# Attention block of a fused kernel: q kept per head with zero rows for the other head, q–k products over 112 rows, a state of 48 columns per pair

## Chip, cores and metric

The kernel runs on one core of a Trainium2 chip. The metric is the time of one execution on the device in microseconds (us). The core has five engines that run side by side, each with its own queue of instructions that it takes strictly in order: PE (TensorE, matrix products into PSUM), DVE (VectorE), ACT (ScalarE), POOL (GpSimd) and SP (here only issuing DMAs). Engines wait for each other through semaphores. PSUM has eight banks; all eight are in use here.

## The reference

Two stages. The first is linear attention with a decaying state, for 4 batches, 8 heads, 768 steps and 48 features per head:

```python
for t in range(S):
    state = alpha[:, :, t, :, None] * state + np.einsum('bhd,bhe->bhde', k[:, :, t], v[:, :, t])
    y[:, :, t] = np.einsum('bhd,bhde->bhe', q[:, :, t], state)
```

The second takes y, laid out as 3072 rows (batch and step) of 384 (heads and features), through a layer with 2048 hidden units:

```python
h = x @ w_in
r = np.maximum(h, 0.0)
g = s * (r * r) + b
return (g @ w_out).astype(np.float32)
```

Inputs and output are fp32. The products in the kernel take bf16 operands and sum in fp32.

## The kernel before

**Tiling.** The steps are cut into 24 blocks of 128 (six per batch, `n` from 0 to 23; `c = n % 6` is the place in the batch). The recurrence is turned into products within a block plus a state carried from block to block. The eight heads are handled as four pairs (`NP = 4`). A pair's features lie at 0 to 47 for the even head and 64 to 111 for the odd head, so that a transposed pair takes 112 rows, of which 48 to 63 are unused.

**One block goes through these functions**, in this order:

- `ln(n)` (L186, ACT): the logarithm of alpha. `vcast(n)` (L189, POOL): v to bf16.
- `cum(n)` (L195 to L211): PE adds the logarithms up over the steps (L195); ACT takes exp of the negative sums (`bi_sb`, L206) and of the sums (`b_sb`, L207). The decay over the whole block, `blast`, comes from PE and ACT for the first five blocks, and otherwise through DRAM by three small DMAs (`decay`).
- `qk(n)` (L223, L224, DVE): k times `bi_sb`, q times `b_sb`, in bf16.
- `tr(n)` (L229 to L237): eight transposes on PE, four pairs of q and four of k, into one bank, `ct_ps`, which `cum` uses too; then one DVE copy of 112x1024 from that bank to `qkT`.
- `amat(n)` (L244, L252): for each pair and head, one product of k and q over that head's 48 rows (0 to 47 or 64 to 111), 128 columns, eight in all. Those of even heads go to one bank (`a_ps[0]`), those of odd heads to another. DVE multiplies each bank with the triangular mask (`am_a`, `am_b`).
- `yp(n)` (L263, L272, L283, L290): y is the sum of the state's part (four products of 112 rows, 96 columns, with the state of the block before, `sd_sb`; none for `c = 0`) and of eight products of `am` and v (48 columns each). Then four products of k and v (96 columns per pair) give the block's addition to the state in `p_ps`. ACT copies y to bf16.
- `st(n)` (L331 to L343): DVE adds the carried state `sc_sb` to `p_ps` (`t1_sb`, 112x384). POOL multiplies with the decay: two instructions for the two heads of the pairs, which write the diagonal 48x48 parts of `sd_sb` in bf16 (its other parts stay at zero from the start), and one of 112x384 for `sc_sb` in fp32. The 96 columns of a pair hold 48 for the even and 48 for the odd head; the parts that mix the two heads are computed and not used.
- `xt(n)` (L311, L317): three transposes of y on PE, and a copy on ACT into `xd_all`.
- The second stage, in four quarters `u`: `mp` (L359, PE, 12 products with w_in of 128 columns into one of two banks `h_ps`), `rl` (L373, relu on ACT), `sq` (L380, square on DVE), and `mm2` (L397, PE, four products with w_out of 384 columns into `o_ps`). In the text these are also called by their names in the list: `m` is `mp`, `rl` and `sq`; `mr` is the first two; `o` is `mm2`. The output of the first 14 blocks is copied out by ACT (L406) and gets its bias later on DVE (L436); that of the others gets it at once on DVE (L410). Blocks 0 and 1 go through the second stage as one group with 256 columns.

**The order is written out by hand.** Every engine's queue has its instructions in the order in which the calls are made. For the first blocks the calls stand in a list; `busy` is filler work on PE that keeps its clock up. From the list, around blocks 1 and 2:

```python
(tr, 1), (ln, 2), (xt, 0), (vcast, 2), (cum, 2), (busy, 1), (amat, 1),
(busy, 3), (yp, 1), (qk, 2), (st, 1), (load_w_in, 1), ..., (busy, 1), (tr, 2), (ln, 3), (xt, 1), (vcast, 3), (cum, 3), (busy, 1), (amat, 2),
(busy, 3), (yp, 2), (qk, 3), (st, 2), (tr, 3), (xt, 2), (mr, 0, 0), (amat, 3), (mr, 0, 1), (mr, 1, 0), (sq, 0, 0), (weights_out,),
```

From block 4 on each call has a due position, with 8 units per block: `cum`, `tr` and `amat` of block `n` run 14.8, 10.8 and 7.9 units ahead of its `yp` in the middle of the run, and the four quarters of the second stage 2.5 to 14.5 units behind it.

**Loads.** SP issues the loads of alpha, k, q and v (192 KB each per block). POOL issues four loads of w_in that convert to bf16: the first behind `st(0)`, three behind `st(1)`. `weights_out` writes one element of `w_out_st` with DVE (L474) so that the loads of w_out, issued by SP (L136), come behind it. w_out is cast in four parts (L143 on DVE, L151 on ACT).

Of the kernel before, what the change touches and what calls it, by code (L numbers as in the profile page):

```python
# [8 lines left out]
FP32 = mybir.dt.float32  # L9
BF16 = mybir.dt.bfloat16  # L10
AF = mybir.ActivationFunctionType
ALU = mybir.AluOpType

@with_exitstack
def kernel(
# [12 lines left out]
    nc = tc.nc  # L28

    B, H, S, D = q.shape  # L30
    C = 128
    NCH = S // C
    NP = H // 2
# [14 lines left out]
    sb = ctx.enter_context(tc.tile_pool(name="sb", bufs=1))  # L48
# [5 lines left out]
    t_ps = ct_ps.bitcast(BF16).rearrange("a (x p t) -> a x p t", x=2, p=NP)  # L54
# [8 lines left out]
    def ring(name, shape, dtype, n):  # L63
        return [sb.tile(shape, dtype, name=f"{name}{i}") for i in range(n)]
# [30 lines left out]
    xd_all = sb.tile([128, UNITS, KT * C], BF16, name="xd_all")  # L95
# [130 lines left out]
    def tr(n):  # L226
        for x, t in ((0, qb_sb[n % 2]), (1, kb_sb[n % 3])):
            for p in range(NP):
                nc.tensor.transpose(  # L229
                    out=t_ps[0:112, x, p, :],  # L230
                    in_=t.rearrange("a h d -> a (h d)")[:, 128 * p : 128 * p + 112],
                    identity=ident,
                )
        nc.vector.tensor_copy(  # L234
            out=qkT_sb[n % 2][0:112].rearrange("a x p t -> a (x p t)"),
            in_=t_ps[0:112].rearrange("a x p t -> a (x p t)"),
        )  # L237

    def amat(n):
        qkT = qkT_sb[n % 2]  # L240
        for p in range(NP):
            for e in range(2):
                r0 = 64 * e
                nc.tensor.matmul(  # L244
                    out=a_ps[e][:, p, :],
                    lhsT=qkT[r0 : r0 + 48, 1, p, :],
                    rhs=qkT[r0 : r0 + 48, 0, p, :],
                    start=True,
                    stop=True,
                )  # L250
        for e in range(2):
            nc.vector.tensor_tensor(out=am_sb[e][n % 2], in0=a_ps[e], in1=mask4, op=ALU.mult)  # L252

    group_of = []
    for g, sz in enumerate(GROUPS):
# [3 lines left out]
    def yp(n):  # L259
        c = n % NCH  # L260
        if c > 0:
            for p in range(NP):
                nc.tensor.matmul(  # L263
                    out=y_ps[:, 96 * p : 96 * p + 96],
                    lhsT=qkT_sb[n % 2][0:112, 0, p, :],
                    rhs=sd_sb[(n - 1) % 2][0:112, p, :],
                    start=(p == 0),
                    stop=False,
                    skip_group_check=True,
                )  # L270
        for h in range(H):
            nc.tensor.matmul(  # L272
                out=y_ps[:, 48 * h : 48 * h + 48],
                lhsT=am_sb[h % 2][n % 2][:, h // 2, :],
                rhs=v_bf[n % 3][:, h, :],
                start=(c == 0 and h == 0),
                stop=(h == H - 1),
                skip_group_check=True,
            )
        if c < NCH - 1:  # L280
            kb = kb_sb[n % 3].rearrange("a h d -> a (h d)")
            for p in range(NP):
                nc.tensor.matmul(  # L283
                    out=pst[:, p, :],
                    lhsT=kb[:, 128 * p : 128 * p + 128],
                    rhs=v_bf[n % 3][:, 2 * p : 2 * p + 2, :],
                    start=True,
                    stop=True,
                )
        nc.scalar.activation(out=y_bf[n % 2], in_=y_ps[:, 0 : H * 48], func=AF.Copy)  # L290
# [233 lines left out]
    for n in range(4, NBLK):  # L524
        p = 8 * n
# [50 lines left out]
```

## Time and profile before

| | us |
|---|---|
| time, median of 3 runs | 194.7 (194.15 to 194.95) |
| the profiled execution: its time | 194.84 |
| the profiled execution: span from the first to the last instruction | 193.1 |

| engine | busy us | share of the span | instructions |
|---|---|---|---|
| PE | 180.4 | 93% | 2380 |
| DVE | 149.1 | 77% | 288 |
| ACT | 117.3 | 61% | 240 |
| POOL | 63.7 | 33% | 100 |

| instruction | count | mean ns |
|---|---|---|
| L234 DVE copy of `qkT`, 112x1024 bf16 | 24 | 683 |
| L244 PE product of q and k, 48 rows, 128 columns | 192 | 222 |
| L263 PE state's part of y, 112 rows, 96 columns | 80 | 205 |
| L272 PE `am` times v, 48 columns | 192 | 185 |
| L333 DVE `t1_sb`, 112x384 fp32 | 16 | 549 |
| L338 POOL `sd_sb`, 48x192 | 40 | 509 |
| L342 POOL `sc_sb`, 112x384 | 16 | 1334 |
| L380 DVE square, 128x512 bf16 | 96 | 506 |
| L373 ACT relu, 128x512 | 90 | 596 |

How to read it: the span is the time between the first and the last instruction of one profiled execution; the time contains 1.7 us around it. PE's matmuls are pipelined: the duration of one (222 ns) is longer than the distance from its start to the next one's start, so what a matmul costs a busy PE is read from the starts, not from the durations. In the rows of the timeline the first number is the start in us, the second the time until the end of the merged rows, then the engine, the line, the operation with its output and inputs, and how many were merged; in brackets stands how long the engine had been idle, and what ended that. In rows of windows the busy us of PE, PE's weight loads, DVE, ACT and POOL follow the length of the window, each with its number of instructions; then the granted clock, the share of DMA and GB/s.

### The profile page before, as it was taken

The numbers are of one execution on the slowest core, as the hardware profiler recorded it, in microseconds if no ns is written. First come the engines' busy times: TensorE is split into PE (matmuls) and PEld (weight loads), VectorE is DVE, ScalarE is ACT, GpSimd is POOL, SyncE is SP. The second block draws the span as 40 slices with busy tenths as digits, with TensorE's granted clock in tenths as the row PEclk, the third lists the DMA queues.
The fourth block names the chain that finished last, engine by engine and source line by source line (L and its number), as shares of the span: only waits on it lengthen the run. The fifth ranks groups of instructions, "written<-read, shape, count | busy, mean of one in ns | idle before, by whom it ended". The sixth has DMA issues, their size and how long they took to land.

```text
span 193.1 us, 5968 instructions
## 1 busy us (share of the span) xinstructions
PE 180.4 (93%) x2380; PEld 143.7 (74%) x2380; DVE 149.1 (77%) x288; ACT 117.3 (61%) x240; POOL 63.7 (33%) x100
## 2 busy tenths in 40 slices
PE   0898897999999999999999999999999999999993
PEld 0575686765867788888887887887887888788782
DVE  5367875488668887988968996688988999998641
ACT  3355387725766586676676677776656657554540
POOL 6146841002310542642411562462202383243000
PEclk9999999999999999999999999999999999999998
DMA  6999999999995684772969277579959474724612
GB/s 122 190 186 185 135 189 350 343 175 190 193 165 90 118 137 70 127 141 37 204 119 159 42 131 126 85 124 163 145 153 197 121 173 122 168 84 156 219 41 82
DMA packets 113453, 28.74 MB, mean 149 GB/s; under 512 B 106627, under 2 KB 113426, under 8 KB 113426
## 3 DMA queue, kind: packets, MB, share of 16 engines
q1 hardware_dynamic: 111822, 26.79, 70.5%
q0 software_dynamic: 1600, 1.57, 5.6%
q8 instruction: 18, 0.29, 0.7%
q14 instruction: 9, 0.07, 0.1%
q10 hardware_dynamic: 4, 0.00, 0.0%
HBM read 25.19 MB, written 4.74 MB: 155 GB/s over the span
## 4 chain that ended last, share of the span: by engine, by line
PE 76%; DVE 5%; DMA 4%; ACT 2%; issue 1%; DVEq 0%; ACTq 0%
PE o_ps L397 28%; PE h_ps L359 28%; PE ct_ps L229 5%; DMA w_out_st<-in_moe_w_out_dram 4%; PE a_ps L244 3%; PE a_ps L397 3%; PE h_ps L311 2%; PE y_ps L272 2%; PE ct_ps L195 2%; PE a_ps L420 1%; PE y_ps L263 1%; ACT r_sb L373 1%; PE p_ps L283 1%; DVE am_b L252 1%; DVE qb_sb L224 1%
## 5 line engine op out<-in xcount | busy, mean ns | idle before, releaser
L373 ACT ACTIVATE r_sb<-h_ps 128x512 bf16<-128x512 f32 x90 | 53.5, 596 | 35.2 <-PE h_ps L359 33.4
L359 PEld LDWEIGHTS <-w_in_bf 128*128 128x128 bf16 x1104 | 67.8, 98 | 6.8 <-issue 0.7
L359 PE MATMUL h_ps<-xd_all,w_in_bf 128*128 128x128 bf16 (+1 forms) x1056 | 71.3, 220 | 0.2 <-ACT xd_all L317 0.2
L397 PE MATMUL o_ps<-w_out_bf,gt_all 128*128 128x384 bf16 x336 | 68.3, 326 | 1.6 <-DVE w_out_bf L143 1.5
L380 DVE TENSOR_TENSOR gt_all<-r_sb 128x512 bf16<-128x512 bf16 x96 | 47.1, 506 | 25.6 <-ACT r_sb L373 25.0
L338 POOL TENSOR_TENSOR sd_sb<-t_sb,blast 48x192 bf16<-48x192 f32 x40 | 20.4, 509 | 77.7 <-DVE t_sb L333 35.4
L397 PEld LDWEIGHTS <-gt_all 128*128 128x128 bf16 x368 | 32.6, 98 | 17.9 <-DVE w_out_bf L143 1.7
L189 POOL CAST v_bf<-v_sb 128x384 bf16<-128x384 f32 x24 | 16.6, 691 | 34.7 <-DMA v_sb<-in_v_dram 33.3
L342 POOL TENSOR_TENSOR sc_sb<-t_sb,blast 112x384 f32<-112x384 f32 x16 | 21.3, 1334 | 1.3
L317 ACT ACTIVATE xd_all<-h_ps 128x384 bf16<-128x384 bf16 x23 | 11.3, 491 | 15.0 <-PE h_ps L311 15.0
L234 DVE COPY qkT<-ct_ps 112x1024 bf16<-112x1024 bf16 x24 | 16.4, 683 | 3.7 <-PE ct_ps L229 3.1
L252 DVE TENSOR_TENSOR am_a<-a_ps,mask 128x512 bf16<-128x512 f32 x24 | 16.4, 683 | 3.4 <-PE a_ps L244 3.4
L223 DVE TENSOR_TENSOR kb_sb<-k_sb,bi_sb 128x384 bf16<-128x384 f32 x24 | 13.8, 575 | 3.9 <-ACT bi_sb L206 3.8
L252 DVE TENSOR_TENSOR am_b<-a_ps,mask 128x512 bf16<-128x512 f32 x24 | 16.3, 679 | 0.0
L224 DVE TENSOR_TENSOR qb_sb<-q_sb,b_sb 128x384 bf16<-128x384 f32 x24 | 15.1, 628 | 0.1
L186 ACT ACTIVATE la_sb<-al_sb 128x384 bf16<-128x384 f32 x24 | 12.4, 517 | 3.8 <-DMA al_sb<-in_alpha_dram 3.8
L290 ACT ACTIVATE y_bf<-y_ps 128x384 bf16<-128x384 f32 x24 | 11.7, 489 | 4.6 <-PE y_ps L272 4.4
L229 PEld LDWEIGHTS <-qb_sb 128*112 128x112 bf16 x96 | 8.8, 136 | 5.0 <-DVE qb_sb L224 3.5
L229 PE MATMUL ct_ps<-ident,qb_sb 128*112 128x128 bf16 x96 | 10.0, 230 | 1.0 <-DVE qb_sb L224 1.0
L206 ACT ACTIVATE bi_sb<-ct_ps 128x384 f32<-128x384 f32 x20 | 9.7, 486 | 1.0 <-PE ct_ps L195 1.0
L244 PE MATMUL a_ps<-qkT 48*128 48x128 bf16 x192 | 9.7, 222 | 0.4 <-DVE qkT L234 0.4
L207 ACT ACTIVATE b_sb<-ct_ps 128x384 f32<-128x384 f32 x20 | 9.9, 495 | 0.0
(75 smaller groups left out, 197.0 us busy)
## 6 DMA issues: line engine op xcount, KB each, us to landing
al_sb<-in_alpha_dram SPq DMA_DIRECT2D x24, 192.0 KB
k_sb<-in_k_dram SPq DMA_DIRECT2D x24, 192.0 KB
q_sb<-in_q_dram SPq DMA_DIRECT2D x24, 192.0 KB
v_sb<-in_v_dram SPq DMA_DIRECT2D x24, 192.0 KB
w_out_st<-in_moe_w_out_dram SPq DMA_DIRECT2D x4, 768.0 KB
out_dram<-w_in_st SPq DMA_DIRECT2D x14, 192.0 KB
out_dram<-out_sb SPq DMA_DIRECT2D x9, 192.0 KB
w_in_bf<-in_moe_w_in_dram POOLq DMA_DIRECT2D x4, 384.0 KB, 6.9
```

The costliest lines, as they stand in the source:

```text
L189: nc.gpsimd.tensor_copy(out=v_bf[n % 3], in_=v_sb[n % NLD])
L224: nc.vector.tensor_tensor(out=qb_sb[n % 2][:, :, 0:48], in0=q_sb[n % NLD], in1=b_sb[n % 3], op=ALU.mult)
L229: nc.tensor.transpose(out=t_ps[0:112, x, p, :], in_=t.rearrange("a h d -> a (h d)")[:, 128 * p : 128 * p + 112], identity=ident,)
L234: nc.vector.tensor_copy(out=qkT_sb[n % 2][0:112].rearrange("a x p t -> a (x p t)"), in_=t_ps[0:112].rearrange("a x p t -> a (x p t)"),)
L244: nc.tensor.matmul(out=a_ps[e][:, p, :], lhsT=qkT[r0 : r0 + 48, 1, p, :], rhs=qkT[r0 : r0 + 48, 0, p, :], start=True, stop=True,)
L252: nc.vector.tensor_tensor(out=am_sb[e][n % 2], in0=a_ps[e], in1=mask4, op=ALU.mult)
L338: nc.gpsimd.tensor_tensor(out=sd[r, :, d], in0=t1_sb[r, :, d], in1=bl[r].to_broadcast([48, NP, 48]), op=ALU.mult)
L342: nc.gpsimd.tensor_tensor(out=sc_sb[0:112], in0=t1_sb[0:112], in1=bl[0:112].to_broadcast([112, NP, 96]), op=ALU.mult)
L359: nc.tensor.matmul(out=hp[:, jj * N : (jj + 1) * N], lhsT=w_in_bf[:, kk, 128 * j : 128 * (j + 1)], rhs=xd_sb[g][:, kk, 0:N], start=(kk == ...
L373: nc.scalar.activation(out=rs, in_=h_of.pop((g, u)), func=AF.Relu)
L380: nc.vector.tensor_tensor(out=gt_sb[g][:, u * 512 : (u + 1) * 512], in0=rs, in1=rs, op=ALU.mult)
L397: nc.tensor.matmul(out=op[:, 0:d_model], lhsT=gt_sb[g][:, j * N + t * C : j * N + (t + 1) * C], rhs=w_out_bf[:, j, :], start=(j == 0), sto ...
```

## The change

k and q are kept apart. k stays transposed by pairs (`kT`, 112 rows). q is kept per head: `qbd` has for each pair two planes of 112 rows and 128 columns, one with the even head's q in rows 0 to 47, the other with the odd head's q in rows 64 to 111; all else is zero, set once at the start (with `t1_sb`, whose rows 48 to 63 are not written otherwise). The one copy from `ct_ps` becomes three: k on DVE, the odd heads' q on ACT, the even heads' q on DVE. `amat` has four products over 112 rows with 256 columns, one per pair; the zero rows keep the two heads apart. The first two pairs go to one bank and the last two to the other, so `am_sb[0]` holds heads 0 to 3. The state has 48 columns per pair: rows 0 to 47 for the even head, 64 to 111 for the odd head. `t1_sb` is made by two DVE instructions of 48x192, `sd_sb` and `sc_sb` by one POOL instruction of 112x192 each. The state's part of y takes eight products of 48 columns.

```diff
-    qkT_sb = ring("qkT", [128, 2, NP, 128], BF16, 2)
+    kT_sb = ring("kT", [128, NP, 128], BF16, 2)
+    qbd_sb = ring("qbd", [128, NP, 2, 128], BF16, 2)
...
-    t1_sb = sb.tile([128, NP, 96], FP32, name="t1_sb")
-    sc_sb = sb.tile([128, NP, 96], FP32, name="sc_sb")
-    sd_sb = ring("sd_sb", [128, NP, 96], BF16, 2)
+    t1_sb = sb.tile([128, NP, 48], FP32, name="t1_sb")
+    sc_sb = sb.tile([128, NP, 48], FP32, name="sc_sb")
+    sd_sb = ring("sd_sb", [128, NP, 48], BF16, 2)
...
-        nc.vector.tensor_copy(
-            out=qkT_sb[n % 2][0:112].rearrange("a x p t -> a (x p t)"),
-            in_=t_ps[0:112].rearrange("a x p t -> a (x p t)"),
-        )
+        nc.vector.tensor_copy(out=kT_sb[n % 2][0:112], in_=t_ps[0:112, 1])
+        nc.scalar.activation(out=qbd_sb[n % 2][64:112, :, 1], in_=t_ps[64:112, 0], func=AF.Copy)
+        nc.vector.tensor_copy(out=qbd_sb[n % 2][0:48, :, 0], in_=t_ps[0:48, 0])
...
         for p in range(NP):
-            for e in range(2):
-                r0 = 64 * e
-                nc.tensor.matmul(
-                    out=a_ps[e][:, p, :],
-                    lhsT=qkT[r0 : r0 + 48, 1, p, :],
-                    rhs=qkT[r0 : r0 + 48, 0, p, :],
-                    start=True,
-                    stop=True,
-                )
+            nc.tensor.matmul(
+                out=a_ps[p // 2][:, 2 * (p % 2) : 2 * (p % 2) + 2, :],
+                lhsT=kT_sb[n % 2][0:112, p, :],
+                rhs=qbd_sb[n % 2][0:112, p],
+                start=True,
+                stop=True,
+            )
...
-            for p in range(NP):
+            for h in range(H):
                 nc.tensor.matmul(
-                    out=y_ps[:, 96 * p : 96 * p + 96],
-                    lhsT=qkT_sb[n % 2][0:112, 0, p, :],
-                    rhs=sd_sb[(n - 1) % 2][0:112, p, :],
+                    out=y_ps[:, 48 * h : 48 * h + 48],
+                    lhsT=qbd_sb[n % 2][0:112, h // 2, h % 2, :],
+                    rhs=sd_sb[(n - 1) % 2][0:112, h // 2, :],
...
-                lhsT=am_sb[h % 2][n % 2][:, h // 2, :],
+                lhsT=am_sb[h // 4][n % 2][:, h % 4, :],
...
-        if c == 0:
-            nc.vector.tensor_copy(out=t1_sb[0:112], in_=pst[0:112])
-        else:
-            nc.vector.tensor_tensor(out=t1_sb[0:112], in0=pst[0:112], in1=sc_sb[0:112], op=ALU.add)
-        bl = blast[n % 3]
-        sd = sd_sb[n % 2]
         for e in range(2):
             r, d = slice(64 * e, 64 * e + 48), slice(48 * e, 48 * e + 48)
-            nc.gpsimd.tensor_tensor(
-                out=sd[r, :, d], in0=t1_sb[r, :, d], in1=bl[r].to_broadcast([48, NP, 48]), op=ALU.mult
-            )
+            if c == 0:
+                nc.vector.tensor_copy(out=t1_sb[r], in_=pst[r, :, d])
+            else:
+                nc.vector.tensor_tensor(out=t1_sb[r], in0=pst[r, :, d], in1=sc_sb[r], op=ALU.add)
+        bl = blast[n % 3][0:112].to_broadcast([112, NP, 48])
+        nc.gpsimd.tensor_tensor(out=sd_sb[n % 2][0:112], in0=t1_sb[0:112], in1=bl, op=ALU.mult)
         if c < NCH - 2:
-            nc.gpsimd.tensor_tensor(
-                out=sc_sb[0:112], in0=t1_sb[0:112], in1=bl[0:112].to_broadcast([112, NP, 96]), op=ALU.mult
-            )
+            nc.gpsimd.tensor_tensor(out=sc_sb[0:112], in0=t1_sb[0:112], in1=bl, op=ALU.mult)
...
-    for t in sd_sb:
+    for t in qbd_sb + [t1_sb]:
         nc.vector.memset(t, 0.0)
```

More of the change, by code (lines that the diff above doesn't have):

```diff
@@ L233, in tr @@
                 )
-        nc.vector.tensor_copy(
-            out=qkT_sb[n % 2][0:112].rearrange("a x p t -> a (x p t)"),
-            in_=t_ps[0:112].rearrange("a x p t -> a (x p t)"),
-        )
+        nc.vector.tensor_copy(out=kT_sb[n % 2][0:112], in_=t_ps[0:112, 1])
+        nc.scalar.activation(out=qbd_sb[n % 2][64:112, :, 1], in_=t_ps[64:112, 0], func=AF.Copy)
+        nc.vector.tensor_copy(out=qbd_sb[n % 2][0:48, :, 0], in_=t_ps[0:48, 0])
     def amat(n):
-        qkT = qkT_sb[n % 2]
         for p in range(NP):
-            for e in range(2):
-                r0 = 64 * e
-                nc.tensor.matmul(
-                    out=a_ps[e][:, p, :],
-                    lhsT=qkT[r0 : r0 + 48, 1, p, :],
-                    rhs=qkT[r0 : r0 + 48, 0, p, :],
-                    start=True,
-                    stop=True,
-                )
-        for e in range(2):
-            nc.vector.tensor_tensor(out=am_sb[e][n % 2], in0=a_ps[e], in1=mask4, op=ALU.mult)
+            nc.tensor.matmul(
[5 more added lines that the diff above has]
+            )
+        for i in range(2):
+            nc.vector.tensor_tensor(out=am_sb[i][n % 2], in0=a_ps[i], in1=mask4, op=ALU.mult)
     group_of = []
@@ L261, in yp @@
         if c > 0:
-            for p in range(NP):
+            for h in range(H):
                 nc.tensor.matmul(
-                    out=y_ps[:, 96 * p : 96 * p + 96],
-                    lhsT=qkT_sb[n % 2][0:112, 0, p, :],
-                    rhs=sd_sb[(n - 1) % 2][0:112, p, :],
-                    start=(p == 0),
+                    out=y_ps[:, 48 * h : 48 * h + 48],
+                    lhsT=qbd_sb[n % 2][0:112, h // 2, h % 2, :],
+                    rhs=sd_sb[(n - 1) % 2][0:112, h // 2, :],
+                    start=(h == 0),
                     stop=False,
```

## The prediction

> **What bounds the kernel now.** The page's first lines and its chain come first: TensorE is busy 93% of the span and holds 76% of the chain that ended last.
>
> ```profile
> PE 180.4 (93%) x2380; PEld 143.7 (74%) x2380; DVE 149.1 (77%) x288; ACT 117.3 (61%) x240; POOL 63.7 (33%) x100
> PE 76%; DVE 5%; DMA 4%; ACT 2%; issue 1%; DVEq 0%; ACTq 0%
> ```
>
> A share hides stages, so I cut the span into windows. Between 45 and 187 us TensorE is the bound; between 25.5 and 34 it is idle a fifth of the time.
>
> ```profile
> 25.50:34.00 8.50, 6.82 (x93) 6.14 (x91) 5.17 (x11) 6.50 (x12) 2.04 (x3) 1.00 1.11 283
> 45.00:187.00 142.00, 140.74 (x1968) 114.05 (x1966) 117.85 (x222) 92.81 (x191) 47.29 (x63) 1.00 0.69 134
> ```
>
> A busy matmul row is no proof of a full engine, so I read the starts. Matmuls of 128, 384 and 48 columns start every 56, 162 and 25 ns there; TensorE waits over 0.18 us only seven times, 2.4 us in all. What lengthens a block on TensorE lengthens the run. The first 34 us are another kind: the chain in order of time leads from DVE to the load of w_out.
>
> ```profile
> 25.52 7.21 DMA w_out_st<-in_moe_w_out_dram
> 32.84 1.03 DVE w_out_bf L143
> 33.92 0.82 PE o_ps L397 x4
> ```
>
> Before it blocks 0 to 3 run one behind another. The timeline from block 1's transposes to block 2's:
>
> ```profile
> 12.35 0.52 ACT L186 ACTIVATE la_sb<-al_sb 128x384 bf16<-128x384 f32 x1
> 12.71 0.63 PE L229 MATMUL ct_ps<-ident,kb_sb 128*112 128x128 bf16 x4
> 13.39 0.69 DVE L234 COPY qkT<-ct_ps 112x1024 bf16<-112x1024 bf16 x1 [0.72 <-PE ct_ps L229]
> 13.46 0.53 PE L195 MATMUL h_ps<-la_sb,U_bf 128*128 128x384 bf16 x1
> 14.62 0.40 PE L244 MATMUL a_ps<-qkT 48*128 48x128 bf16 x8
> 15.05 0.69 DVE L252 TENSOR_TENSOR am_a<-a_ps,mask 128x512 bf16<-128x512 f32 x1 [0.97 <-PE a_ps L244]
> 16.25 0.55 DVE L223 TENSOR_TENSOR kb_sb<-k_sb,bi_sb 128x384 bf16<-128x384 f32 x1
> 17.32 0.43 PE L229 MATMUL ct_ps<-ident,qb_sb 128*112 128x128 bf16 x4 [0.20 <-DVE qb_sb L224]
> ```
>
> The first row matters most: ln(2) ran on ScalarE at 12.35, before block 1's transposes were done (13.35), so cum(2) at 13.46 found its input.
>
> **The change, part by part.** Sums are against the profiled execution, 194.84 us (span 193.1 and 1.7 around it), 0.14 above the median of the three runs shown.
>
> *Copies in the first blocks.* One DVE copy of 1024 columns (0.69) becomes kT of 512, a ScalarE copy of 48x512, and a DVE copy of 48x512. DVE rows of 384 and 1024 columns from this kind of source, and bf16 rows of 512, put the 512-column copy near 0.42 (halving the part that grows of 0.69 over a fixed 0.15). ScalarE's row of 512 columns takes 0.60, its next instruction starts 0.5 behind it. No row shows two engines reading one bank at once. If ScalarE may read beside DVE, its copy ends 0.65 after the transposes, no later than the old one; if it waits for kT, 0.05 + 0.42 + 0.05 + 0.60 = 1.1 after them. The nearest rows are the exps, masks and copies, of which no two engines read one bank together; I take the wait. The Trainium skill, "PSUM — Partial Sum Buffer", section "PSUM bank collisions raise a hardware error", says that two engines must not touch one bank in the same 32 partitions at once; by it the wait is there for the shared rows 64 to 111, and DVE's last copy may run beside ScalarE.
>
> The copy itself lengthens transposes-to-amat by 0.38. Its place costs more. It is issued in tr(n), so it stands on ScalarE's queue in front of ln(n+1), and behind that are cum(n+1) on PE and, in PE's order, amat(n).
> - Block 0: amat(0) 0.38 later; at the clock of the first 14.5 us (matmuls of 512 columns start 0.43 apart, later 0.22) four matmuls of 256 take 0.85, where amat(0) to cum(1) took 0.54. cum(1) and all behind it: 0.68 late.
> - Block 1: transposes end at 13.35 + 0.68 = 14.03; kT to 14.5, the ScalarE copy holds the queue to 15.04, ln(2) ends 15.55, cum(2) at 15.6 instead of 13.46. From cum to amat takes 0.57 at the later clock (17.98, filler 18.33, 0.22 more): amat(1) at 16.17 instead of 14.62, **1.55** late.
> - Block 2: 2.70 from amat(1) to tr(2) as before: 18.87, end 19.53, then 0.04 + 0.42 + 0.05 + 0.5 + 0.52 + 0.05 to cum(3), 0.57 to amat(2) at 21.7 instead of 18.76: **2.9** late. Here t1 in two halves (0.35 each for 192 columns, where 384 took 0.55) fits into DVE's wait for the transposes (0.28 before) nearly.
> - Block 3 has no ln behind its copies: 0.38 more, amat(3) **3.3** late, 26.2.
>
> Not all of it reaches the end. From amat(3) to the first matmul with w_out took 22.91 to 33.92, of which 1.62 was waiting for w_out. PE comes there at 26.2 + 9.4 = 35.6. w_out must be there by then: its load is issued behind the first gt, 25.52 + 3.3, less 0.47, since that gt took 0.89 beside POOL's sc and 0.42 alone: 28.3. Its data began at 28.33 when w_in's ended; w_in is issued by POOL behind state 1, 19.81 before. That state's t1 is 1.7 late, POOL's own part falls from 1.08 + 0.83 to 0.5 + 0.5, so w_in and its data come 0.7 later. An issue takes 0.83 to its first packet (187.47 to 188.30), so w_out starts at 29.4, 1.1 late; DVE, free at 34.2, casts until 35.2, before PE arrives. **First stage: +1.7.**
>
> *Products of q and k.* In the middle of the run, block 9's rows:
>
> ```profile
> 82.80 0.33 PE L283 MATMUL p_ps<-v_bf,kb_sb 128*128 128x96 bf16 x4
> 83.06 0.40 PE L244 MATMUL a_ps<-qkT 48*128 48x128 bf16 x8
> 83.39 0.82 PE L397 MATMUL o_ps<-w_out_bf,gt_all 128*128 128x384 bf16 x4
> ```
>
> From 82.80 to 83.39 is 0.59; four matmuls of 96 columns start 0.042 apart (0.17), so the eight products cost 0.42. They start in pairs every 56 ns, 0.23 of the 0.42; about 0.095 of idle stands on either side. The new four have 256 columns; rows of that width start 0.109 apart (six from 25.12, next at 25.77): 0.436. Rows of 112 partitions (L263) have no idle before or after, so I give the new ones none: +0.012, 20 blocks, +0.24. The Trainium skill, "TensorEngine Tiling (Array Packing)", sections "Theoretical Speedup" and "Key Properties", speaks against the change: a product over 64 rows or fewer can run two at a time, which is given up here; but a change of tiling mode drains the engine. By the first rule alone the sum would be 0.21 more per block; the idle on both sides agrees with the second.
>
> *State part of y.* Four matmuls of 96 columns (0.172 to the next) become eight of 48 at the 25 ns of L272: 0.20. +0.03 in 17 blocks: **+0.5**. Their weight loads, four more, hide as L272's do.
>
> *DVE, POOL, ScalarE in the middle.* DVE gets 0.08 per block for the copies and 0.15 to 0.23 for t1. POOL's two sd of 0.50 and an sc of 0.83 (1.57 beside DVE) become two of 0.5. That frees DVE: the square L380 takes 0.42 alone and 0.75 on average beside POOL. So DVE's load hardly grows. ScalarE gets 0.5 to 0.6 per block, 8% of its time:
>
> ```profile
> 80.89 0.68 DVE L234 COPY qkT<-ct_ps 112x1024 bf16<-112x1024 bf16 x1
> 81.36 0.60 ACT L373 ACTIVATE r_sb<-h_ps 128x512 bf16<-128x512 f32 x1 [1.17 <-PE h_ps L359]
> 83.22 0.49 ACT L290 ACTIVATE y_bf<-y_ps 128x384 bf16<-128x384 f32 x1
> 84.05 0.33 PE L311 MATMUL h_ps<-ident,y_bf 128*128 128x128 bf16 x3
> ```
>
> Its copy falls into the wait of 1.17; behind it stand relu, a copy of o, ln, relu, y_bf, nearly without gaps, and PE waits for y_bf at 84.05, 0.33 after it ends. With kT done at 81.1 to 81.3 the copy pushes the relu by 0.2 to 0.4 and y_bf by 0.1 to 0.3: inside the cover, just. Without cover it is 0.2 to 0.5 per block. amat comes 0.6 to 1.7 after qkT, more than the 0.38 added. Blocks 5 to 7 lie tight (y_bf, la and am_b waits of 0.2 to 0.6): I add 0.6 there and take off 0.4 of the waits at 139.8 (0.28) and 164.5 (0.36), which lie behind POOL-slowed DVE work: **+0.2**.
>
> The memsets at the start (two of 512 words, one of 192, for two of 192) end by 4.3; DVE's next work is at 5.83. Nothing.
>
> Sum: 1.7 + 0.24 + 0.5 + 0.2 = 2.6; 194.84 + 2.6 = **197.5**.
>
> **Rivals.**
> 1. *ScalarE doesn't wait for kT, or PE's filler hides more.* Each queue step loses 0.4; amat(3) is 1.9 late, o follows w_in's and w_out's data, about +0.8. With the rest 196.2 to 196.5. Chance 0.18.
> 2. *The gain on POOL decides: not slower.* If ln(n+1) is done before ScalarE reaches the copy, or is not held by it, POOL issues w_in 0.7 earlier, w_out lands 0.6 earlier, and 1.6 of PE's wait shrinks by that; with 0.64 of waits gone against 0.74 of PE work: 194.2 to 194.8. It decides from the point where amat(3) is under 1.6 late. Against it: ScalarE's instructions are in the order of the code in every row I read. Chance 0.14.
> 3. *The middle stalls.* kT late on a loaded DVE (0.4 to 1.2 behind the transposes in six blocks) holds ScalarE, y_bf misses its 0.33: 0.3 in 17 blocks, +5: 202 to 203. Chance 0.12.
> 4. *The 112-row products keep the idle on both sides:* 0.19 in 20 blocks, +3.8: 201. Chance 0.05.
>
> **How the numbers follow.** The forecast has 0.51: 197.5, itself 196.6 to 199.0, the top if PE's clock rises one step later for the idle time around 14.5. The range 195.7 to 200.2 leaves out rival 2, most of 3, and 4's half. Within 0.5% is about what a measurement here can tell from no change: 193.7 to 195.7. Slower: forecast, rivals 3, 4 and nearly all of 1, 0.83; same 0.14; faster 0.03.
>
> **What would show it.** In the new profile: ln(2) and ln(3) behind the ScalarE copy, cum(2) near 15.6; amat(3) near 26; w_out issued near 28.3 and the first o near 35.6; amat with no idle around it, 0.44; y's state part 0.20; squares beside POOL rarer; y_bf still ended before xt's transposes. I am wrong if ScalarE's ln runs ahead, or if PE waits for y_bf in most blocks.

## The result, and the profile after

The changed kernel takes **205.79 us** (median of 6 runs, 204.87 to 206.46), the kernel before in the same batch 194.31 (194.09 to 194.95): ratio **1.0574**, 95% interval 1.0549 to 1.0599. The forecast of 197.5 had the sign right and the size wrong: 11.5 us slower, not 2.8, and outside the range. The profiled execution took 204.90 (span 203.1), 10.06 more than that of before.

First the page's busy times and its chain, as before:

```profile
PE 183.6 (90%) x2364; PEld 146.0 (72%) x2364; DVE 149.9 (74%) x333; ACT 130.1 (64%) x264; POOL 35.8 (18%) x80
PE 62%; DVE 7%; ACT 7%; DMA 7%; issue 3%; SPq 1%; POOL 0%; ACTq 0%; POOLq 0%
```

No engine became the bound by its load: PE has 3 us more, DVE 1, ACT 13 at a share of 64%, POOL 28 less. What changed is that PE waits. The 7% of DMA in the chain are the decay's row, a load of q and one of k between 59 and 73 us, and the decay again from 159; none of the waits of PE that the profile lists between 45 and 187 us ends at a DMA. The window of 45 to 187 us, as before:

```profile
45.00:187.00 142.00, 136.80 (x1836) 109.43 (x1835) 112.94 (x247) 99.16 (x204) 22.77 (x47) 1.00 0.72 132
```

PE is idle there for 5.20 us, where it was idle for 1.26. Where the time goes can be read off the starts of the transposes of q in the two timelines. The rows are the stretches from block to block (us; block 4 counts from the start of the span):

| stretch | before | after | more |
|---|---|---|---|
| start to block 4 | 42.83 | 45.06 | 2.23 |
| block 4 to 8 | 23.07 | 25.54 | 2.47 |
| block 8 to 14 | 41.97 | 44.70 | 2.73 |
| block 14 to 17 | 21.78 | 21.99 | 0.21 |
| block 17 to 23 | 42.47 | 44.77 | 2.30 |

These make up 9.94 of the 10.06 us. So a fifth is lost ahead of block 4, near the forecast, and nearly all of the rest in the middle, where the forecast saw about 1.

**First blocks.** The timeline around block 1's transposes, in place of the rows of before from 12.35 on:

```profile
13.84 0.42 DVE L235 COPY kT<-ct_ps 112x512 bf16<-112x512 bf16 x1
14.30 0.59 ACT L236 ACTIVATE qbd<-ct_ps 48x512 bf16<-48x512 bf16 x1 [1.06 <-DVE kT L235]
14.92 0.52 ACT L187 ACTIVATE la_sb<-al_sb 128x384 bf16<-128x384 f32 x1
14.92 0.42 DVE L237 COPY qbd<-ct_ps 48x512 bf16<-48x512 bf16 x1 [0.66 <-ACT qbd L236]
15.49 0.32 PE L196 MATMUL h_ps<-la_sb,U_bf 128*128 128x384 bf16 x1 [1.56 <-ACT la_sb L187]
16.05 0.60 PE L241 MATMUL a_ps<-qbd,kT 112*128 112x256 bf16 x4
```

`ln(2)` (L187) stands behind ScalarE's copy, as foreseen, and `cum(2)` waits for it. What was not foreseen is the second DVE row: it starts only when ScalarE's copy has ended. The three copies run strictly one behind another, 1.5 us for 0.42 + 0.59 + 0.42 of work. It is so in all 24 blocks, by the page's groups:

```profile
L236 ACT ACTIVATE qbd<-ct_ps 48x512 bf16<-48x512 bf16 x24 | 14.2, 592 | 27.6 <-DVE kT L235 27.6
L237 DVE COPY qbd<-ct_ps 48x512 bf16<-48x512 bf16 x24 | 10.0, 416 | 17.3 <-ACT qbd L236 17.3
```

The chain in order of time no longer leads over the load of w_out. It leads over block 3's copies (ScalarE's at 25.61, DVE's last at 26.23) and its products of q and k (26.70) to the first matmul with w_out, which starts at 36.22 (33.92 before).

**Middle.** The same timeline from block 10's transposes to block 11's, PE, ACT and DVE rows of one round:

```profile
85.99 0.43 PE L230 MATMUL ct_ps<-ident,qb_sb 128*112 128x128 bf16 x4
...
86.69 0.42 DVE L235 COPY kT<-ct_ps 112x512 bf16<-112x512 bf16 x1
87.20 0.59 ACT L236 ACTIVATE qbd<-ct_ps 48x512 bf16<-48x512 bf16 x1 [1.18 <-DVE kT L235]
87.82 0.60 ACT L365 ACTIVATE r_sb<-h_ps 128x512 bf16<-128x512 f32 x1
...
89.10 0.60 ACT L365 ACTIVATE r_sb<-h_ps 128x512 bf16<-128x512 f32 x1
...
89.73 0.42 DVE L372 TENSOR_TENSOR gt_all<-r_sb 128x512 bf16<-128x512 bf16 x1 [0.29 <-ACT r_sb L365]
90.07 0.73 DVE L332 TENSOR_TENSOR t_sb<-p_ps,sc_sb 48x192 f32<-48x192 f32 x2
...
90.84 0.69 DVE L249 TENSOR_TENSOR am_a<-a_ps,mask 128x512 bf16<-128x512 f32 x1
...
92.04 0.73 DVE L224 TENSOR_TENSOR kb_sb<-k_sb,bi_sb 128x384 bf16<-128x384 f32 x1
...
92.69 0.55 DVE L225 TENSOR_TENSOR qb_sb<-q_sb,b_sb 128x384 bf16<-128x384 f32 x1
...
93.29 0.43 PE L230 MATMUL ct_ps<-ident,qb_sb 128*112 128x128 bf16 x4
```

Read as one round this is a **closed loop**. The transposes of block 10 release kT; ACT copies q and only then runs its relu of quarter 2; behind it on ACT stand a copy of o, `ln` and the relu of quarter 3 (89.10); DVE waits for that relu, squares it, and only behind the square come t1, the two masks, kb and qb (for block 11), for which block 11's transposes wait. The same round in the kernel before (its relu of quarter 2, at 81.36, stands in the prediction):

```profile
79.98 0.39 PE L229 MATMUL ct_ps<-ident,qb_sb 128*112 128x128 bf16 x4
...
83.37 0.42 DVE L380 TENSOR_TENSOR gt_all<-r_sb 128x512 bf16<-128x512 bf16 x1 [0.61 <-ACT r_sb L373]
83.71 0.55 DVE L333 TENSOR_TENSOR t_sb<-p_ps,sc_sb 112x384 f32<-112x384 f32 x1
...
84.18 0.68 DVE L252 TENSOR_TENSOR am_a<-a_ps,mask 128x512 bf16<-128x512 f32 x1
...
85.38 0.55 DVE L223 TENSOR_TENSOR kb_sb<-k_sb,bi_sb 128x384 bf16<-128x384 f32 x1
...
85.84 0.55 DVE L224 TENSOR_TENSOR qb_sb<-q_sb,b_sb 128x384 bf16<-128x384 f32 x1
```

Each step, from its start to the next, before and after (the 0.60 of before is qb's 0.55 and a hand-over; PE itself came later, at 87.02):

| step | before | after |
|---|---|---|
| transposes to relu of quarter 2 | 79.98 to 81.36: 1.38 | 1.83 |
| to square of quarter 3 (over ACT: o, ln, relu) | to 83.37: 2.01 | 1.91 |
| to t1 | to 83.71: 0.34 | 0.34 |
| to the first mask | to 84.18: 0.47 | 0.77 |
| over the second mask to kb | to 85.38: 1.20 | 1.20 |
| to qb | to 85.84: 0.46 | 0.65 |
| to the earliest next transpose | 0.60 | 0.60 |
| sum | **6.46** | **7.30** |

PE's own work for a block is 7.04 before (79.98 to 87.02). So the loop had 0.58 to spare then, and nothing in PE's waits told of it. After, PE's work is 7.08 by this count (the forecast's 0.01 and 0.03 on top), the loop is 7.30, and the blocks start 7.30 apart. That a chain from one block's transposes to the next adds up to their distance is no proof that it sets the pace; the experiments test that. One sign is in the table already: blocks 14 to 17 took 7.26 each before, with PE busy throughout, and they became only 0.07 longer each.

### The profile page after: what moved, and what is told of

Same layout as the page of the kernel before. It is cut to its first block, busy times and chain, and to the rows that moved or that the text cites. A ratio compares the mean times of both kernels' runs of the same rounds, so it can differ in the third digit from the quotient of the medians.

```text
span 203.1 us, 5996 instructions
## 1 busy us (share of the span) xinstructions
PE 183.6 (90%) x2364; PEld 146.0 (72%) x2364; DVE 149.9 (74%) x333; ACT 130.1 (64%) x264; POOL 35.8 (18%) x80
## 4 chain that ended last, share of the span: by engine, by line
PE 62%; DVE 7%; ACT 7%; DMA 7%; issue 3%; SPq 1%; POOL 0%; ACTq 0%; POOLq 0%
PE h_ps L351 21%; PE o_ps L389 21%; PE ct_ps L230 5%; ACT r_sb L365 3%; PE a_ps L241 3%; PE a_ps L389 3%; DMA row_dr<-b_sb 2%; PE h_ps L308 2%; DMA k_sb<-in_k_dram 2%; DMA q_sb<-in_q_dram 2%; PE y_ps L269 2%; PE a_ps L412 1%; ACT qbd L236 1%; PE ct_ps L196 1%; PE y_ps L260 1%
## 5 line engine op out<-in xcount | busy, mean ns | idle before, releaser
L372 DVE TENSOR_TENSOR gt_all<-r_sb 128x512 bf16<-128x512 bf16 x96 | 39.2, 423 | 19.9 <-ACT r_sb L365 19.8
L334 POOL TENSOR_TENSOR sd_sb<-t_sb,blast 112x192 bf16<-112x192 f32 x20 | 10.3, 514 | 123.1 <-DVE t_sb L330 38.9
L236 ACT ACTIVATE qbd<-ct_ps 48x512 bf16<-48x512 bf16 x24 | 14.2, 592 | 27.6 <-DVE kT L235 27.6
L237 DVE COPY qbd<-ct_ps 48x512 bf16<-48x512 bf16 x24 | 10.0, 416 | 17.3 <-ACT qbd L236 17.3
L224 DVE TENSOR_TENSOR kb_sb<-k_sb,bi_sb 128x384 bf16<-128x384 f32 x24 | 16.1, 672 | 2.8 <-ACT bi_sb L207 2.8
L190 POOL CAST v_bf<-v_sb 128x384 bf16<-128x384 f32 x24 | 12.7, 533 | 27.7 <-DMA v_sb<-in_v_dram 27.7
L241 PE MATMUL a_ps<-qbd,kT 112*128 112x256 bf16 x96 | 14.9, 277 | 2.2 <-DVE qbd L237 2.2
L187 ACT ACTIVATE la_sb<-al_sb 128x384 bf16<-128x384 f32 x24 | 12.5, 521 | 1.8 <-DMA al_sb<-in_alpha_dram 1.7
L235 DVE COPY kT<-ct_ps 112x512 bf16<-112x512 bf16 x24 | 10.1, 421 | 3.4 <-PE ct_ps L230 1.8
L241 PEld LDWEIGHTS <-kT 112*128 112x128 bf16 x96 | 8.5, 98 | 4.4 <-issue 2.3
L332 DVE TENSOR_TENSOR t_sb<-p_ps,sc_sb 48x192 f32<-48x192 f32 x32 | 11.2, 351 | 0.5
```

Of the source, the lines that this page charges most:

```text
L187: nc.scalar.activation(out=la_sb[n % 2][:, :, 0:48], in_=al_sb[n % NLD], func=AF.Ln)
L190: nc.gpsimd.tensor_copy(out=v_bf[n % 3], in_=v_sb[n % NLD])
L224: nc.vector.tensor_tensor(out=kb_sb[n % 3][:, :, 0:48], in0=k_sb[n % NLD], in1=bi_sb[n % 2], op=ALU.mult)
L236: nc.scalar.activation(out=qbd_sb[n % 2][64:112, :, 1], in_=t_ps[64:112, 0], func=AF.Copy)
L241: nc.tensor.matmul(out=a_ps[p // 2][:, 2 * (p % 2) : 2 * (p % 2) + 2, :], lhsT=kT_sb[n % 2][0:112, p, :], rhs=qbd_sb[n % 2][0:112, p], sta ...
L372: nc.vector.tensor_tensor(out=gt_sb[g][:, u * 512 : (u + 1) * 512], in0=rs, in1=rs, op=ALU.mult)
```

## The experiments

Theory A: the hand-over of one q copy to ScalarE costs the time, either because that copy stands ahead of the relu on ScalarE's queue (A1), or because DVE's last copy waits behind it (A2). Theory B, the rival: the state in halves of 48 columns, with more and longer DVE instructions, costs it. Theory C: PE's new products cost it. The results in one place; each ratio is against the kernel before in the same batch, with its 95% interval; "apart" is the distance of the transposes of blocks 10 and 11, "first o" the start of the first matmul with w_out:

| run | median us | ratio | first o | apart |
|---|---|---|---|---|
| change | 205.79 | 1.0574 (1.0549 to 1.0599) | 36.22 | 7.30 |
| e1_dve_copies | 196.88 | 1.0111 (1.0076 to 1.0146) | 34.46 | 7.12 |
| e2_dve_first | 213.62 | 1.0970 (1.0941 to 1.0999) | 38.18 | 7.65 |
| e3_old_state | 209.26 | 1.0759 (1.0718 to 1.0799) | 37.00 | 7.59 |
| e4_before_act_copy | 215.65 | 1.1074 (1.1034 to 1.1114) | 37.83 | 7.84 |
| e5_before_state48 | 195.43 | 1.0064 (1.0041 to 1.0086) | 33.34 | 7.16 |
| e6_old_products | 196.56 | 1.0122 (1.0087 to 1.0158) | 34.13 | 7.12 |
| e7_ln_ahead | 204.45 | 1.0530 (1.0495 to 1.0566) | 35.62 | 7.30 |
| e8_act_later | 206.36 | 1.0628 (1.0591 to 1.0664) | 35.65 | 7.64 |
| e9_square_later | 203.83 | 1.0437 (1.0361 to 1.0514) | 37.63 | 7.08 |
| e10_ln_earlier | 203.14 | 1.0411 (1.0344 to 1.0477) | 36.25 | 7.07 |
| e11_both | 202.40 | 1.0379 (1.0313 to 1.0444) | 36.37 | 7.08 |
| e12_before_ln_earlier | 194.40 | 0.9976 (0.9950 to 1.0002) | 34.12 | 7.10 |
| e13_before_both | 195.97 | 1.0037 (0.9978 to 1.0095) | 34.36 | 7.14 |
| e14_dve_copies_both | 195.68 | 1.0047 (1.0026 to 1.0067) | 34.55 | 7.07 |
| e15_act_later_both | 197.86 | 1.0163 (1.0135 to 1.0191) | 35.15 | 7.07 |
| e16_state48_both | 193.63 | 0.9951 (0.9938 to 0.9964) | 33.26 | 7.04 |

The kernel before has its first o at 33.92 and its blocks 7.04 apart. The last two columns are each from one profiled execution. The first o depends on the granted clock as well: in most profiles it is 1.00 from 15 to 30 us, but in stretches of 5 us it is 0.67, 0.84 and 0.80 in e2, 0.76, 0.50 and 0.72 in e4, and 0.66 from 20 to 25 us in e9. e9, e10 and e11 have the first stage of the change; at the full clock it ends within 0.15 us of the change's 36.22, in e9 1.4 later.

### Which part of the change costs the time

**e1_dve_copies**: the change, with all three copies on DVE.

```diff
-        nc.scalar.activation(out=qbd_sb[n % 2][64:112, :, 1], in_=t_ps[64:112, 0], func=AF.Copy)
         nc.vector.tensor_copy(out=qbd_sb[n % 2][0:48, :, 0], in_=t_ps[0:48, 0])
+        nc.vector.tensor_copy(out=qbd_sb[n % 2][64:112, :, 1], in_=t_ps[64:112, 0])
```

> The change, with the odd heads' q copied by DVE too (three copies on DVE, none on ACT). Theory A (the hand-over DVE to ACT to DVE on one bank makes the loop of a block longer than PE's work): copies end 1.1 us after the transposes instead of 1.6, ln is no longer behind them, ACT is free: 197 to 199.5 us, blocks in the middle 7.05 to 7.15 apart. Theory B (the state's two half instructions and DVE's work decide): DVE has even more work, 204 or more. Theory C (PE's new products decide): no change, 204 to 206.

Measured 196.88: 8.9 of the 11.5 us go with the hand-over, although DVE now has 162.1 us of work instead of 149.9. The same copy costs less on the busier engine. Theory C falls: PE's new products are all still there.

**e3_old_state**: the change with the state of before (96 columns per pair, t1 in one instruction, two `sd` on POOL).

```diff
+    t1_sb = sb.tile([128, NP, 96], FP32, name="t1_sb")
...
+    sd_sb = ring("sd_sb", [128, NP, 96], BF16, 2)
...
+                    rhs=sd_sb[(n - 1) % 2][0:112, h // 2, 48 * (h % 2) : 48 * (h % 2) + 48],
...
+            nc.vector.tensor_tensor(out=t1_sb[0:112], in0=pst[0:112], in1=sc_sb[0:112], op=ALU.add)
```

> The change, with the state of before (96 columns per pair, one t1 of 112x384 on DVE, two sd and an sc of 112x384 on POOL); products and copies as in the change. Theory A (copies): within 2 us of the change, 203.5 to 207 us, DVE's squares slowed by POOL again. Theory B (the state's halves on DVE): 200 us or less.

Measured 209.26, above what either theory gave: theory B falls, and A's range missed too. With the copies as in the change, the new state saves 3.5 us; with the old one DVE's squares take 506 ns on average again, not 423.

**e6_old_products**: e1 with the eight products over 48 rows, out of kT and the padded q.

```diff
+            for e in range(2):
+                r0 = 64 * e
+                nc.tensor.matmul(
+                    out=a_ps[e][:, p, :],
+                    lhsT=kT_sb[n % 2][r0 : r0 + 48, p, :],
+                    rhs=qbd_sb[n % 2][r0 : r0 + 48, p, e],
...
```

> The version with three DVE copies (196.9 us), with eight products of q and k over 48 rows and 128 columns instead of four over 112 rows and 256 columns (the masks by even and odd heads as before). By the idle on both sides of the old products, the two forms cost the same within 0.013 us per block: 196.3 to 197.2 us. If two at a time were worth what it saves in columns, 0.2 us per block less: 192 to 193.5 us.

Measured 196.56, against e1's 196.88 with intervals that overlap nearly whole: no difference between the two forms of the products is measurable (each interval is 0.7 us wide to either side).

**e4_before_act_copy**: the kernel before, plus one ScalarE copy of the odd heads' q behind the DVE copy. Nothing reads its result; nothing is left out.

```diff
+        nc.scalar.activation(out=extra_sb[n % 2][64:112], in_=t_ps[64:112, 0], func=AF.Copy)
```

> The kernel before, with one ACT copy of 48x512 from the transposes' bank added behind the copy to qkT; nothing reads what it writes. Theory A1 (ACT's queue): its place ahead of ln and relu costs without any wait of DVE: 199 to 204 us, amat(3) 2 us or more late. Theory A2 (DVE's wait behind ACT): 196 us or less, since no DVE instruction waits for it.

Measured 215.65, 21 us more for 24 copies of 0.59, beyond what any theory gave; no wait of DVE behind ScalarE is needed for it. Of the 20.9 us between the profiled executions 3.9 arise ahead of block 4, where the granted clock was lower too, and 16.2 from there to block 23. Its middle timeline shows how (DVE's two squares, ScalarE's copy, and xt's transposes on PE):

```profile
89.14 1.68 DVE L382 TENSOR_TENSOR gt_all<-r_sb 128x512 bf16<-128x512 bf16 x2
...
91.52 0.59 ACT L239 ACTIVATE extra<-ct_ps 48x512 bf16<-48x512 bf16 x1 [1.73 <-DVE qkT L235]
...
94.44 0.34 PE L313 MATMUL h_ps<-ident,y_bf 128*128 128x128 bf16 x3 [0.47 <-ACT y_bf L292]
```

Two squares beside POOL take 1.68 (1.41 in the kernel before) and hold the DVE copy, which holds ScalarE's, which ends 2.5 after the transposes (89.58). The relu, ln and y_bf come late behind it and PE waits for y_bf in every quiet block: here the round closes over y_bf and PE (transposes to xt 4.86, xt to the next transposes 2.98, together 7.84). That is rival 3's mechanism, in a kernel that is not the change.

**e5_before_state48**: the kernel before with only the state changed: t1 and `sc` of 48 columns per pair, two `sd` into the diagonal parts.

```diff
+        for e in range(2):
+            r, d = slice(64 * e, 64 * e + 48), slice(48 * e, 48 * e + 48)
...
+                nc.vector.tensor_tensor(out=t1_sb[r], in0=pst[r, :, d], in1=sc_sb[r], op=ALU.add)
```

> The kernel before, with the state of 48 columns alone: t1 in two halves of 48x192 on DVE, two sd of 48x192 into the diagonal parts, one sc of 112x192; copies, products and y as before. PE's work is the same. If POOL's shorter sc frees DVE's squares and that takes away some of the 2.4 us of waits: 193 to 194.5 us. If the second t1 instruction on DVE costs more than that gives: 195 to 197 us.

Measured 195.43, 0.6% slower, with quiet blocks 7.16 apart: alone, the second t1 instruction costs more than POOL's relief gives. t1's +0.30 by itself would use up only half of the 0.58 to spare. But with POOL's `sc` shorter, its cast of v begins 5.81 behind the transposes (7.04 before) and comes to lie beside qb, which takes 0.85, not 0.55. Added up as above, from the transposes at 79.70: 1.42 to the relu, 2.01 to the square, then 0.34, 0.77, 1.21, 0.50, and 0.91 from qb to the next transposes at 86.86, together 7.16. The loop is full here too.

### What about the hand-over costs it

**e2_dve_first**: the change with DVE's q copy ahead of ScalarE's, so that DVE waits for no one.

```diff
-        nc.scalar.activation(out=qbd_sb[n % 2][64:112, :, 1], in_=t_ps[64:112, 0], func=AF.Copy)
         nc.vector.tensor_copy(out=qbd_sb[n % 2][0:48, :, 0], in_=t_ps[0:48, 0])
+        nc.scalar.activation(out=qbd_sb[n % 2][64:112, :, 1], in_=t_ps[64:112, 0], func=AF.Copy)
```

> The change, with DVE's copy of the even heads' q ahead of ACT's copy, so that DVE waits for nobody between its two copies; ACT's copy starts about 0.34 us later than in the change. Theory A1 (what costs is ACT's queue: relu and y_bf late behind its copy): 205 to 208 us. Theory A2 (what costs is DVE's wait of 0.66 us per block behind ACT's copy): 199 to 202 us, squares and masks earlier.

Measured 213.62, worse than the change and than A2 or A1 gave. A2 falls as the cause in the middle: what counts there is when ScalarE gets free. Its copy starts 1.56 behind the transposes (90.39 to 91.95), 1.21 in the change, and the blocks are longer by the same 0.35: 7.65 instead of 7.30.

**e8_act_later**: DVE's two copies first, ScalarE's issued by a call of its own, behind `ln` in the first blocks and behind the relu of quarter 2 in the middle.

```diff
+    def qhi(n):
+        nc.scalar.activation(out=qbd_sb[n % 2][64:112, :, 1], in_=t_ps[64:112, 0], func=AF.Copy)
...
+            at(p - t + 0.5, qhi, n)
```

> The change, with ACT's copy called later: behind ln in the first blocks, behind the next relu in the middle; DVE's two copies at the old place. The same work on every engine. Theory A1 (the place in ACT's queue, relu held behind a copy that waits for DVE): 197 to 200.5 us. If ACT's 0.6 us more per block costs wherever it stands: 203 us or more.

Measured 206.36: no gain, and A1 in its plain form falls as well. The relu of quarter 2 is on time again, yet blocks are 7.64 apart. Its timeline, ACT and DVE:

```profile
87.32 0.60 ACT L367 ACTIVATE r_sb<-h_ps 128x512 bf16<-128x512 f32 x1 [1.40 <-PE h_ps L353]
87.94 0.59 ACT L239 ACTIVATE qbd<-ct_ps 48x512 bf16<-48x512 bf16 x1
...
89.36 0.59 ACT L367 ACTIVATE r_sb<-h_ps 128x512 bf16<-128x512 f32 x1
...
89.97 0.42 DVE L374 TENSOR_TENSOR gt_all<-r_sb 128x512 bf16<-128x512 bf16 x1 [1.44 <-ACT r_sb L367]
```

The copy is still between the two relus; DVE waits 1.44 for the second one. Added up as in the table above (transposes at 85.90): 1.42 to the relu, 2.65 to the square, then 0.35, 0.76, 1.21, 0.65 and 0.60: **7.64**, and the next transposes are at 93.54. This gave the **loop theory**: it does not matter where in the loop ScalarE's 0.6 lies. It predicts that anything of that size taken out of the loop, with no work removed, gives the time back.

**e7_ln_ahead**: `ln(1)` to `ln(3)` called ahead of `tr(0)` to `tr(2)`, for the first stage alone. The list's second line, as an example:

```diff
-            (busy, 3), (yp, 0), (qk, 1), (st, 0), (load_w_in, 0), (busy, 1), (tr, 1), (ln, 2), (xt, 0), (vcast, 2), (cum, 2), (busy, 1), (amat, 1),
+            (busy, 3), (yp, 0), (qk, 1), (st, 0), (load_w_in, 0), (busy, 1), (ln, 2), (tr, 1), (xt, 0), (vcast, 2), (cum, 2), (busy, 1), (amat, 1),
```

> The change, with ln(1), ln(2) and ln(3) called ahead of tr(0), tr(1) and tr(2), so that ACT does not have them behind its copy. If ln's place makes the first stage late: amat(3) at 24 to 25 us instead of 26.7 and the first product with w_out 1 to 1.5 us earlier, the middle as in the change, 203.8 to 205 us. If the copies' length makes it late: amat(3) after 26, 205 to 206.5 us.

Measured 204.45, first o at 35.62, 0.6 earlier, amat(3) at 26.11 (26.70 in the change, 22.91 before) where 24 to 25 was expected. So ln's place is only the smaller part of the first stage's loss. That the rest is the length of the three copies in a row is argued, not shown; e1, whose copies in a row are shorter, loses 0.5 there instead of 2.3. The middle is as in the change (7.30), as it should be.

### Taking work out of the loop

**e9_square_later** calls the square of quarter 3 behind `qk`, **e10_ln_earlier** calls `ln` 2.6 units earlier, ahead of the transposes, and **e11_both** does both; the rest is the change. The first pair of lines is that of `ln`, the others that of the square:

```diff
-            at(p - c - 1.9, ln, n)
+            at(p - c - 4.5, ln, n)
...
-            at(p + (2.5, 3.5, 5.5, 7.5)[u], m, group_of[n][0], u)
+            if u == 3 and n < NBLK - 1:
+                at(p + 7.5, mr, group_of[n][0], 3)
+                at(p + 9.6, sq, group_of[n][0], 3)
+            else:
+                at(p + (2.5, 3.5, 5.5, 7.5)[u], m, group_of[n][0], u)
```

> The change, with the square of the last quarter (u = 3) called behind the next qk instead of ahead of the state and the masks. The same work. Loop theory: a block is 7.30 us long because tr, kT, ACT's copy, two relus with a copy and ln between them, the square, t1, masks, kb and qb follow one another until the next tr (6.46 us before, 0.84 longer now, and PE's work is 7.09); with the square out of it DVE no longer waits for the second relu, and blocks fall to 7.09 to 7.15: 200 to 203 us. If it is DVE's or ACT's amount of work and not the loop: 205 to 206.5 us.

> The change, with ln called 2.6 units earlier from block 5 on, into ACT's idle stretch ahead of the third quarter's relu instead of between the two relus. The same work. Loop theory: 0.41 us leave the loop of 7.30, PE's 7.09 is the bound again, and y_bf is earlier for xt: 199.5 to 202.5 us. Otherwise 205 to 206.5 us.

> The change with both moves, ln earlier and the last square later. Loop theory: no more than 1 us below the better one of the two, since PE bounds both; first stage as in the change: 199 to 201.5 us.

Measured 203.83, 203.14 and 202.40. That is 2.0 to 3.4 us less than the change, and all three lie above the ranges expected. In all three the quiet blocks are 7.07 to 7.08 apart, PE's own pace. In e10's timeline `ln` (91.60) stands ahead of ScalarE's copy, and the relus are 0.91 apart, not 1.28:

```profile
91.60 0.51 ACT L187 ACTIVATE la_sb<-al_sb 128x384 bf16<-128x384 f32 x1
...
93.28 0.60 ACT L365 ACTIVATE r_sb<-h_ps 128x512 bf16<-128x512 f32 x1
...
94.19 0.60 ACT L365 ACTIVATE r_sb<-h_ps 128x512 bf16<-128x512 f32 x1
```

The loop is shown there, but only there: e11 is 42.43 in blocks 8 to 14 (41.97 before), and still 24.52 in blocks 4 to 8 (23.07) and 44.86 in blocks 17 to 23 (42.47). In its last blocks PE waits for DVE's `out_sb` (L402), 0.30 to 0.52 in five blocks, 1.9 in all, and this instruction stands on DVE behind the q copy that waits 0.72 for ScalarE.

**e15_act_later_both**: e8 with both moves. Its diff is that of e8 and that of e11 together. It has all the work of the change; DVE's copy no longer stands behind ScalarE's.

> The version with ACT's copy later in its queue and DVE's two copies first (206.4 us), with both moves. The same work as in the change; no DVE instruction waits for ACT's copy. If DVE's wait behind ACT's copy is what is left: waits of the products with w_out for DVE in blocks 18 to 22 (2.7 us) go, 198 to 200 us. If ACT's added work is: 201 to 203 us, y_bf late for xt.

Measured 197.86: **7.9 us less than the change, with the same instructions in another order**. Blocks 8 to 14 take 42.30, blocks 17 to 23 42.19, both as before or nearly; the profile lists no wait of PE for `out_sb`. Against e11, blocks 17 to 23 are 2.67 shorter and the stretch ahead of block 4 is 1.23 shorter. Left over the kernel before are 1.15 ahead of block 4 and 1.62 from there to block 8.

**Controls.** The two moves on kernels without the hand-over: **e12_before_ln_earlier** (before, ln alone), **e13_before_both** (before, both), **e14_dve_copies_both** (e1, both). Their diffs are the two pairs above.

> The kernel before with ln called 2.6 units earlier from block 5 on. Loop theory: its loop of 6.46 us is shorter than PE's 7.04 already, so only some of the few single waits (for y_bf 0.57 and 0.21, for qb 0.36) can go: 193.5 to 194.8 us.

> The kernel before with both moves, ln earlier and the last square later. Loop theory: the loop of 6.46 us does not bound it, PE's 7.04 does: 193.3 to 194.8 us, no clear difference.

> The version with three DVE copies (196.9 us) with both moves. Loop theory: its middle already runs at PE's 7.12 per block, so at most some single waits go: 195.5 to 196.9 us.

Measured 194.40, 195.97 and 195.68. e12's and e13's intervals hold 1: where the loop has room, the moves bring nothing that can be told (e13's median lies above the range expected). On e1 they bring 1.2 us, by the two medians; its quiet blocks go from 7.12 to 7.07.

**e16_state48_both**: the kernel before with e5's state and both moves, by the diffs shown there.

> The kernel before with the 48-column state alone (195.4 us) and both moves. If the second t1 instruction costs by the loop: back to 193.5 to 194.7 us. If by DVE's work as such: 195 to 196 us.

Measured 193.63 (10 runs), ratio 0.9951 (0.9938 to 0.9964): faster than both kernels by a little. e5's loss of 0.6% becomes a gain of 0.5% as soon as the second t1 instruction does not lie on a full loop; the squares take 428 ns on average, nearly as in the change (423).

## Why the prediction was wrong

- **Products of q and k: right.** The forecast was 0.436 without idle; from the first of the four products of k and v at 88.88 to the matmul with w_out at 89.49 is 0.61, less 0.17 for those four, as in the forecast: 0.44. Rival 4, idle on both sides, did not occur, and e6 shows no measurable difference between the old products and the new.
- **State part of y: right**, 0.206 against 0.20.
- **POOL and DVE's load: right.** POOL is down from 63.7 to 35.8, the squares from 506 to 423 ns, DVE's load almost the same. But the loads were not what decided.
- **First stage: +1.7 forecast, +2.3 measured, for a reason only partly right.** amat(1) and amat(2) came at 16.05 and 21.70 (forecast 16.17 and 21.7), amat(3) at 26.70 (26.2), w_out's issue at 28.8 (28.3). The near hit has luck in it. The sum put most of the delay on ln's place, and e7 shows that to be worth about 0.6 at the end. The copies themselves, one behind another, were priced too low: amat(0) came 0.67 late instead of 0.38, and from block 3's transposes to amat(3) it took 0.86 more instead of 0.38. Two errors covered each other.
- **"DVE's last copy may run beside ScalarE": wrong in 24 of 24 blocks.** This was drawn from the Trainium skill, "PSUM — Partial Sum Buffer", section "PSUM bank collisions raise a hardware error", which keeps apart only accesses to the same 32 partitions of a bank. The two copies read rows 0 to 47 and 64 to 111, which share no such group of 32. The trace shows the wait nevertheless, 17.3 us in all. The two copies also write one tile, and no run here separates a wait for the bank from one for the tile. Whether the chip would let them run together was not tried either.
- **The failed step is "DVE, POOL, ScalarE in the middle", +0.2.** With the two terms on PE the forecast had 0.94 behind the first o; it came to 7.8. As those two terms hold, this step came to about 7.0 instead of 0.2. Each wait was held against its own cover, and each looked covered: the copy's push of the relu by 0.2 to 0.4 (0.45 measured), t1's 0.15 to 0.23 (0.30), 0.19 in kb and qb, where kb takes 0.73, not 0.55, beside POOL's cast of v, which comes earlier since POOL's `sc` is shorter. That these lie on one round that ends at the transposes where it began, so that they add up against one slack of 0.58, was not looked for. PE's row of waits before could not show it, because a loop shorter than PE's block leaves no wait.
- **The price of being over** is also more than the 0.22 per quiet block (7.30 less 7.08). Blocks 4 to 8 and 17 to 23 cost +2.47 and +2.30 us. In the former ScalarE's q copy stands ahead of `xd_all` and of y_bf, and PE waits 0.90 (59.66) and 1.06 (67.18) for them; in the latter the late DVE makes PE wait twice for `out_sb`, 1.0 in all. Of the latter, e1 and e15 show that the hand-over's order is the cause; of the former, e1 removes nearly all (23.40), e15 only a third (24.69). In e15 PE still waits there 0.63 for ScalarE's q copy itself (53.32) and 0.86 for y_bf (65.25), which stands on ScalarE behind that copy and a relu.
- **Rivals.** 1 and 2 did not occur: ScalarE waited for kT in every block. Rival 3 had the nearest time, 202 to 203 at a chance of 0.12, by y_bf alone. PE waited for y_bf in four blocks between 45 and 187 us, 2.2 us in all (0.4 before); the quiet blocks were set by the loop over DVE, which no rival named. The sign that the prediction gave for being wrong, waits for y_bf in most blocks, did not come.

## What to carry to other kernels

Before pricing an added instruction wait by wait, follow one block's dependences round until they come back to where they began, across the engines' queues, and hold the round's length against the bound engine's time per block: here 6.46 against 7.04 left 0.58 for all additions together, and 0.84 came. Price what comes to lie side by side, too: in e5 t1's 0.30 became 0.70, as the relief on POOL moved its cast beside qb. A loop that is over can be mended without removing work, by calling something that need not be in it (here `ln`, a square, a copy) earlier or later: e15 has the change's instructions and takes 7.9 us less. A copy handed to a less busy engine was paid here by its place in the queue and by the hand-over itself, not by that engine's share.

## What the runs showed of the hardware

- **Two DVE instructions on different first rows did not overlap.** t1's halves (rows 0 to 47, then 64 to 111) end 0.73 after the first began, and the mask behind them starts 0.77 after it, 0.04 after their end; in the kernel before the mask started 0.08 ahead of t1's end (0.47 after a start, with a duration of 0.55). In e1 the copies of rows 0 to 47 and of rows 64 to 111 did not overlap either (75.17 behind an end at 75.16), while the first of them began 0.08 ahead of the end of kT's, which starts at row 0 as it does. The Trainium skill, "VectorE: DVE Perf Modes", section "Two Vector instructions with no wait between them", says that a DVE instruction whose operand starts in another quadrant than the last one's is held until the earlier ones have ended. The trace agrees; splitting t1 costs 0.30 per block here, of which 0.15 to 0.23 were foreseen.
- **A DVE instruction beside POOL.** Squares of 128x512 in bf16 take 0.42 alone; in e4 a pair of them beside POOL's `sc` and cast takes 1.68 from the first start to the last end.
- **The added ScalarE copy.** 24 copies of 0.59, 14.2 us of work on an engine busy 61% of the time, cost 21 us as an addition (e4), and 8.9 (the change against e1) or 2.2 (e15 against e14) on ScalarE instead of DVE. What differs is where they stand and what waits behind them; in e4 the lower granted clock of the first stage is in it as well.
